# Attention scores of two heads: from 128-row products with moved halves to 64-row products in the two halves of the array

## The chip, the cores and the metric

The kernel runs on one core of a Trainium2 chip, as one launch. The metric is device time in microseconds (us), the median of several executions. TensorE (PE) multiplies matrices: it loads a stationary operand of up to 128 rows by 128 columns (LDWEIGHTS, listed as PEld) and streams a moving operand through it, into PSUM. VectorE (DVE), ScalarE (ACT) and GpSimd (POOL) do the rest, and DMA queues, most of them fed by SyncE (SP), move data.

## What is computed

Attention for 4 batches of 8 heads, 576 positions and 64 values per head, with a bias on the scores that a small network makes from positions; then a mixture of eight experts, in which each token goes to one expert.

```python
B, H, S, D = q.shape                      # 4, 8, 576, 64
scores = scale * np.matmul(q, k.transpose(0, 1, 3, 2))   # scale = 1/8
...
h = np.maximum(x @ w1 + b1, 0.0)          # x from positions alone
bias = h @ w2
scores = scores + bias.transpose(2, 0, 1)[None, :, :, :]
scores = scores - np.max(scores, axis=-1, keepdims=True)
attn = np.exp(scores)
attn = attn / (np.sum(attn, axis=-1, keepdims=True) + 1e-09)
return np.matmul(attn, v).astype(np.float32)
...
for e in range(E):                        # 8 experts, each token to one
    h = np.maximum(x[mask] @ w1[e], 0.0)
    ye = h @ w2[e]
    out[mask] = gate_w[mask, None] * eom[mask, e, None] * ye
```

## The kernel before

Heads are worked on in 16 pairs (batch b, pair pr of heads). The program has three stages. In the **bias stage** 36 steps (emit_hid, emit_bias) make the bias tiles: ACT and DVE make hidden rows (L724, L726), PE multiplies them (L737), ACT empties PSUM (L741) into one of four buffers, and SP writes those into the bias tiles by DMA (L747, L750). Table BEGIN (L66) hangs the first steps of pairs 0 to 2 on these 36 steps. Then comes the **attention stage**: FIRST (pair 0), ORDER (pairs 1 to 14) and LAST (pair 15) are strings that give the order of all steps by hand; one pass of the string serves one pair, a "-" after a step's name means the pair before, a "+" the pair after, "++" two after. Each engine does its instructions in the order in which the steps are emitted. At the end is the **expert stage** (body, from L1107): eight slots of 192 products.

The steps that matter here, for one pair:

- l (emit_load, L760): two DMAs bring keys and queries; each 128-column block of the tile nat has 64 key values and 64 query values of one head side by side.
- k0 k1 k2 (emit_kq, L800): three PE transposes each (L805) put keys in the upper 64 rows and queries in the lower 64. ACT writes the rounded part ("hi", with the scale 1/8 on the queries' rows, L808) and DVE the rest ("lo", L810).
- p0 p1 p2 (emit_place, L814): four DMAs of 288 KB inside the core move halves, so that the tile kt has the keys' hi in both halves, kl the keys' lo in both, and qs the queries' hi above their lo.
- s0 to s7 (emit_s, L842): scores of 128 queries of one head, by four products of 128 rows and 288 columns (L855): each contracts hi and lo of the queries at once, so four partial products go in two passes for each half of the columns. Then softmax_rows: one DVE instruction adds the bias and finds the row maximum (L835), and an ACT exponential follows (L840). The PSUM tile ps has two buffers, one per head.
- s8 (emit_s4, L862): the last 64 queries of both heads in one tile, by eight products (L871), from q4, which POOL fills (z, emit_q4).
- t (emit_t): transposes of the exponentials (L892, L904), emptied by ACT or DVE as the last letter says (L896, L907).
- a (emit_av, L909): twenty products with 64 stationary columns, whose outputs lie in the two column halves of the array (L924).
- w, u, x, y: pieces of routing, storing and of the experts' preparation.

## Time and profile before

| | us |
|---|---|
| median of 3 runs | 616.68 (616.17 to 617.11) |
| the profiled execution | 616.42 |
| its span | 614.5 |
| PE busy in the span | 575.9 |
| DVE busy | 413.7 |
| ACT busy | 375.0 |

The profiled execution took 1.9 us beyond its span and lies 0.26 us under the median. Busy time counts overlapping instructions once; a PE that is listed as busy may still be between two streams, so the start times of its instructions are read, not their durations.

### The profile page before, as it was taken

To read this page: it belongs to the slowest core of one execution; us is meant where nothing else is said; L and a number is where in the kernel's file an instruction comes from. 1 tells how busy PE (TensorE), PEld (TensorE's weight loads), DVE (VectorE), ACT (ScalarE), POOL (GpSimd) and SP (SyncE) were. 2 spreads that over 40 slices of the span, in tenths; PEclk is the share of its full clock that TensorE was granted. 3 is DMA by queue.
4 is the path that set the end of the run, shared out by engine and by line. 5 is a ranking of instruction groups with operands and counts; after the bars stand their busy time and mean duration, and the time that the engine had idled before them with its cause. 6 is when DMAs were issued, how large, how long until landed. Compare 5 with 4: busy or idle time off the path is not lost.

```text
span 614.5 us, 13532 instructions
## 1 busy us (share of the span) xinstructions
PE 575.9 (94%) x5070; PEld 489.2 (80%) x5070; DVE 413.7 (67%) x974; ACT 375.0 (61%) x774; POOL 96.1 (16%) x172
## 2 busy tenths in 40 slices
PE   4878789999999999999989999999999999999993
PEld 2323478887887788887778768999999999999993
DVE  6968756676786677786579765757778675555521
ACT  5778767777775677776776654545445454545510
POOL 1000000000001000100012372040404032230202
PEclk9979989999999999999999999999999999999997
DMA  6998975555656745676436666566656574757621
GB/s 139 228 206 209 219 159 121 130 127 110 142 127 169 169 102 107 134 192 148 103 88 158 190 209 207 158 221 198 209 173 213 169 215 159 232 163 215 187 73 47
DMA packets 99093, 100.26 MB, mean 163 GB/s; under 512 B 71319, under 2 KB 71575, under 8 KB 99016
## 3 DMA queue, kind: packets, MB, share of 16 engines
q1 hardware_dynamic: 93028, 84.93, 54.4%
q0 software_dynamic: 3232, 9.64, 5.0%
q10 hardware_dynamic: 2756, 4.72, 2.2%
q8 instruction: 42, 0.69, 0.5%
q14 instruction: 35, 0.29, 0.2%
HBM read 60.34 MB, written 9.50 MB: 114 GB/s over the span
## 4 chain that ended last, share of the span: by engine, by line
PE 79%; DVE 7%; DMA 5%; ACT 4%; issue 3%; POOL 0%; POOLq 0%; SPq 0%; DVEq 0%; ACTq 0%
PE p L1116 16%; PE p L1137 16%; PE pa L924 13%; PE ps L855 10%; PE pt L892 9%; PE pb L737 2%; DVE hid L726 2%; PE pt L805 2%; PE ps L871 2%; DMA bias<-evh 2%; DVE e L835 2%; PE pt L657 1%; PE pt L1156 1%; PE pt L904 1%; PE pt L515 1%
## 5 line engine op out<-in xcount | busy, mean ns | idle before, releaser
L840 ACT ACTIVATE e<-e,nm 128x576 f32<-128x576 f32 x144 | 111.3, 774 | 49.1 <-DVE nm L835 47.2
L835 DVE CUSTOM_DVE_ANT_0 e<-ps,bias 128x576 f32<-128x576 f32 x144 | 105.6, 751 | 31.1 <-PE ps L855 26.9
L1116 PE MATMUL p<-x,w 128*128 128x288 f32 x768 | 105.9, 297 | 0.0
L1116 PEld LDWEIGHTS p<-x,w 128*128 128x128 f32 x768 | 102.8, 188 | 0.5 <-issue 0.4
L892 PE MATMUL pt<-kept,e 128*128 128x128 f32 x576 | 82.7, 277 | 2.9 <-ACT et L896 1.2
L855 PE MATMUL ps<-qt,qs 128*128 128x288 f32 x256 | 80.0, 331 | 3.3 <-DVE nm L835 2.9
L892 PEld LDWEIGHTS pt<-kept,e 128*128 128x128 f32 x576 | 65.2, 141 | 17.8 <-issue 7.6
L1137 PE MATMUL p<-hh,w2h 128*128 128x288 f32 x256 | 77.3, 302 | 0.0
L1137 PE MATMUL p<-hl,w2h 128*128 128x288 f32 x256 | 75.6, 295 | 0.1
L1137 PE MATMUL p<-hh,w2l 128*128 128x288 f32 x256 | 75.3, 294 | 0.0
L924 PE MATMUL pa<-et,vt 128*64 128x256 f32 (+1 forms) x640 | 73.2, 354 | 0.0
L855 PE MATMUL ps<-kl,qs 128*128 128x288 f32 x256 | 71.4, 296 | 0.0
L896 ACT COPY et<-pt 128x512 f32<-128x512 f32 (+1 forms) x105 | 57.3, 565 | 12.1 <-PE pt L892 11.9
L737 PE MATMUL pb<-hid,w2blk 128*32 128x288 f32 x576 | 47.7, 442 | 17.6 <-DVE hid L726 8.3
L924 PEld LDWEIGHTS pa<-et,vt 128*64 128x64 f32 x640 | 42.6, 137 | 21.9 <-issue 6.1
L855 PEld LDWEIGHTS ps<-qt,qs 128*128 128x128 f32 x256 | 48.8, 191 | 7.2 <-DVE nm L835 4.5
L1118 ACT ACTIVATE hh<-p 128x288 fp32r<-128x288 f32 x64 | 26.3, 412 | 46.2 <-PE p L1116 28.4
L1081 POOL DMA_INDIRECT out_dram<-y,sidx x22 | 26.4, 1199 | 176.4 <-DVE y L1159 150.0
L737 PEld LDWEIGHTS pb<-hid,w2blk 128*32 128x32 f32 x576 | 19.0, 116 | 42.4 <-DVE hid L726 11.0
L726 DVE TENSOR_SCALAR hid<-e,early 128x576 f32<-128x576 f32 x110 | 48.5, 515 | 6.3 <-PE pb L737 2.8
L855 PEld LDWEIGHTS ps<-kl,qs 128*128 128x128 f32 x256 | 49.0, 191 | 0.0
L487 DVE TENSOR_TENSOR w2l<-w2r,w2h 128x1024 fp32r<-128x1024 f32 x32 | 39.2, 1226 | 14.2 <-ACT w2h L486 12.7
(218 smaller groups left out, 972.5 us busy)
## 6 DMA issues: line engine op xcount, KB each, us to landing
w1r<-in_moe_w_dram SPq DMA_DIRECT2D x36, 512.0 KB, 5.1
w2r<-in_moe_w_dram SPq DMA_DIRECT2D x36, 512.0 KB, 4.1
kl<-qs SPq DMA_DIRECT2D x32, 288.0 KB, 5.2
nat<-in_k_dram SPq DMA_DIRECT2D x16, 288.0 KB, 4.2
nat<-in_q_dram SPq DMA_DIRECT2D x16, 288.0 KB, 5.2
bias<-evh SPq DMA_DIRECT2D x16, 288.0 KB, 4.2
bias<-evl SPq DMA_DIRECT2D x16, 288.0 KB, 5.3
qs<-qt SPq DMA_DIRECT2D x16, 288.0 KB, 3.2
```

The source lines that it names most:

```text
L487: V.tensor_tensor(out=lo, in0=src, in1=hi.bitcast(F32), op=ALU.subtract)
L726: V.tensor_scalar(out=to, in0=src, scalar1=bc[:, r:r + 1], scalar2=0.0, op0=ALU.add, op1=ALU.max,)
L737: nc.tensor.matmul(pb[32 * t:32 * t + 32, c, 0:288], lhsT=w2f, rhs=hids[t][:, c * 288:c * 288 + 288], start=True, stop=True,)
L835: V.tensor_tensor_reduce(out=e.rearrange("p (a j) -> p a j", a=2), in0=ps[:, :, 0:n], in1=bias_ap.rearrange("p (a j) -> p a j", a=2), scal ...
L840: nc.scalar.activation(out=e, in_=e, func=ACTF.Exp, scale=-1.0, bias=nm, accum_out=sum_ap)
L855: nc.tensor.matmul(ps[:, c, 0:288], lhsT=qs[:, o:o + 128], rhs=keys[:, k0 + c * 288:k0 + c * 288 + 288], start=n == 0, stop=n == 1,)
L892: nc.tensor.transpose(pt[:, n * 256 + j * 128:n * 256 + j * 128 + 128], es[j][:, (n0 + n) * 128:(n0 + n) * 128 + 128], ident,)
L896: copy(out=et[:, n0:n0 + nn, :].rearrange("p n s -> p (n s)"), in_=pt[:, 0:nn * 256])
L924: nc.tensor.matmul(pa[p:p + 64, 0:n], lhsT=values, rhs=weights, start=i == 0, stop=i == 4)
L1081: p = nc.gpsimd.indirect_dma_start(out=out, out_offset=bass.IndirectOffsetOnAxis(ap=idx, axis=0), in_=y[0:n], in_offset=None, bounds_check ...
L1116: nc.tensor.matmul(p1[:, 0:CH], lhsT=w[:, fs], rhs=x[:, c, :], start=n == 0, stop=n == 11)
L1137: nc.tensor.matmul(p2[:, 0:CH], lhsT=w[f // 2][:, f % 2, ds], rhs=x[f], start=n == 0, stop=n == 23)
```

## The change

Keys and queries of the two heads now stand in different halves: the load puts both heads side by side, so that the transposes leave head 0 in rows 0 to 63 and head 1 in rows 64 to 127, keys and queries in different columns. Nothing needs to be moved after that, and emit_place with its four DMAs is gone. The loads are six DMAs for the same bytes. The scores are three products of 64 rows (hi x hi, hi x lo, lo x hi; lo x lo is dropped) for each half of the columns and each head, and those of head 0 and head 1 alternate. The last 64 queries stay products of 128 rows (q4 is block diagonal), six in place of eight. The scale 1/8 moves into the DVE instruction of the softmax, and the bias tiles are made 8 times larger.

The steps are cut anew: s0 to s3 are both heads of 128 queries and emit only the products; m0 to m3 emit the softmax of both; s4 and m4 are the last 64 queries; k0 to k2 emit transposes and hi, h0 to h2 emit lo. Keys are prepared for the next pair and not for the one after it. In the bias stage, the heads of pair 0 that are begun there are still done one at a time (s00, s10, s01, s11). Which engine empties a transpose changes for several t steps.

```diff
 ORDER = (
-    "s2 s1 c w u a0d- t10a- p0+ s3 u w t11a- s0 u t12a- s6 t20d- p1+ u s7 b- t04d u s8 t01d t03a u "
-    "t02a s5 s4 z+ u w w g- a1a- t14d u p2+ t13a t00d u k0++ a2a- v+ t21d u k1++ w k2++ u l+++ "
+    "l++ s0 b- c t10a- w t12a- m0 u t13d- k2+ s1 u t14a- m1 h2+ u t21d- a0d- w u w u w g- s2 z t20a- t01a t03a m2 u "
+    "t02d u a2d- w s3 u k1+ k0+ t00a m3 u s4 w m4 u t04a h1+ h0+ u a1d- v+ t11d u "
 )
 FIRST = (
-    "s4 t04d t01d s5 t03a t02a s6 t00d s7 v+ s8 t14d z+ k0++ t13a k1++ t21d k2++ l+++"
+    "l++ s2 z m2 t01a t03a t02d s3 m3 t00a v+ s4 m4 t04a t11d"
 )
 LAST = (
-    "b- B W s2 s1 c a0d- u t10a- w s3 u t11a- u s0 t12a- u s6 w t20d- s7 u g- t04d u t01d y t03a s8 u y "
-    "t02a a1a- y s5 X t00d w y s4 a2d- y t14d t13d y a0d t21d w y t12d u y t20d u "
+    "b- B W s0 c t10a- u w t12a- m0 u t13d- u s1 t14a- m1 u t21d- a0d- w u s2 z t20a- g- m2 a1a- u t01a t03a w u y "
+    "t02d u s3 y t00a m3 u X y t04d s4 y a2d- m4 w y t11d t13a y a0d u t14d t12a y y w t21d u t20d u "
 )
...
 BEGIN = {
-    3: "k0", 4: "k1", 5: "k2 l", 7: "p0", 9: "p1", 13: "p2 K0", 14: "z", 16: "K1", 17: "s0", 20: "K2",
-    21: "L", 22: "s2 s1", 29: "P0", 32: "s3 P1", 35: "v P2",
+    3: "k0", 4: "k1", 5: "k2 l", 13: "K0", 16: "K1", 17: "s00", 20: "K2",
+    22: "s10 s01", 32: "s11", 35: "v",
 }
...
-    c["cinv"] = np.stack([1.0 / psi[first + 4 * (q // NE)].astype(np.float64) for q in range(128)])
+    c["cinv"] = np.stack([8.0 / psi[first + 4 * (q // NE)].astype(np.float64) for q in range(128)])
...
         def emit_load(b, pr):
-            t = nat_t[b, pr] = nat.tile([128, 9, 2, D], F32, name="nat", tag="nat")
+
+            t = nat_t[b, pr] = (nat, kq)[pr % 2].tile([128, 9, 2, D], F32, name="nat", tag="nat")
             for i, x in enumerate((k, q)):
+                for hl in range(2):
+                    nc.sync.dma_start(
+                        out=t[:, 5 * i:5 * i + 4, hl, :],
+                        in_=x[b, 2 * pr + hl, 0:512].rearrange("(n p) d -> p n d", p=128),
+                    )
...
-            nc.scalar.activation(out=hi, in_=pt[:, 0:384], func=ACTF.Copy, scale=cn("ksc"))
-            yield
-            V.scalar_tensor_tensor(
-                out=lo, in0=pt[:, 0:384], scalar=cn("ksc"), in1=hi.bitcast(F32), op0=ALU.mult, op1=ALU.subtract
-            )
-
-        def emit_place(b, pr, i):
-
-            hi, lo = (t[(b * NPAIR + pr) % 2] for t in (kh2, qs2))
-            if i == 0:
-                kl_t[b, pr] = kq.tile([128, 2 * S], F32R, name="kl", tag="kt")
-            kl, up, down = kl_t[b, pr], slice(0, 64), slice(64, 128)
-            for to, src in (((kl[up], lo[up]), (kl[down], lo[up])), ((lo[up], hi[down]),), ((hi[down], hi[up]),))[i]:
-                nc.sync.dma_start(out=to.bitcast(F32), in_=src.bitcast(F32))
+            nc.scalar.copy(out=hi, in_=pt[:, 0:384])
+            yield
+            V.tensor_tensor(out=lo, in0=pt[:, 0:384], in1=hi.bitcast(F32), op=ALU.subtract)
...
+        def products(b, pr, qb, heads, outs):
+
+            high, low = (t[(b * NPAIR + pr) % 2] for t in (high2, low2))
+            for c in range(2):
+                for i, (t, keys) in enumerate(((0, high), (0, low), (1, high))):
+                    qs = (high, low)[t]
+                    for hl in heads:
+                        p = slice(hl * 64, hl * 64 + 64) if qb < 4 else slice(0, 128)
+                        nc.tensor.matmul(
+                            outs[hl][:, c, 0:288],
+                            lhsT=qs[p, S + 64 + qb * 128:S + 192 + qb * 128] if qb < 4 else q4[:, t, :],
+                            rhs=keys[p, c * 288:c * 288 + 288], start=i == 0, stop=i == 2,
+                        )
...
-                scale=-1.0, scalar=3.0e38, op0=ALU.add, op1=ALU.min, accum_out=nm,
+                scale=-0.125, scalar=3.0e38, op0=ALU.add, op1=ALU.min, accum_out=nm,
...
-        def emit_s(b, pr, qb, hl):
-            h = 2 * pr + hl
+        def emit_s(b, pr, qb, heads=(0, 1)):
...
             e_t[b, pr, qb] = e_all[qb]
...
+            ps = {hl: ps_s.tile([128, 2, 512], F32, name="ps", tag="s") for hl in heads}
+            products(b, pr, qb, heads, ps)
+            yield
+            for hl in heads:
+                h = 2 * pr + hl
+                softmax_rows(e_t[b, pr, qb][:, hl, :], ps[hl], bias[qb][:, h, :], sums_t[b][:, qb, h:h + 1])
```

## Rows read from the trace of the kernel before

**Rows 1.** Page, parts 1 and 4: busy time; the chain that ended last, by engine.

```profile
PE 575.9 (94%) x5070; PEld 489.2 (80%) x5070; DVE 413.7 (67%) x974; ACT 375.0 (61%) x774; POOL 96.1 (16%) x172
...
PE 79%; DVE 7%; DMA 5%; ACT 4%; issue 3%; POOL 0%; POOLq 0%; SPq 0%; DVEq 0%; ACTq 0%
```

**Rows 2.** The chain in order of time: start us, us, what; pair 1, then later pairs.

```profile
92.77 1.16 PE ps L871 x8
93.93 1.31 PE pt L892 x12
95.24 1.06 PE ps L855 x8
96.30 2.31 PE pa L924 x20
...
105.42 0.59 PE pt L892 x4
106.01 0.53 PE ps L855 x4
106.54 0.44 PE pt L892 x4
...
109.66 0.45 PE ps L871 x3
...
271.48 1.10 PE ps L871 x8
...
303.93 0.75 DVE e L835
...
352.55 1.05 PE ps L871 x8
```

**Rows 3.** Busy time by stretch: us, busy us (instructions) of each engine, clock, DMA.

```profile
core 0: us, PE busy (x) PEld busy (x) DVE busy (x) ACT busy (x) POOL busy (x), PEclk, DMA share, GB/s
92.77:109.66 16.89, 16.86 (x151) 14.11 (x152) 11.52 (x29) 12.76 (x30) 0.99 (x4) 1.00 0.61 132
...
0.00:84.00 84.00, 61.99 (x669) 30.50 (x669) 61.91 (x146) 62.12 (x102) 3.83 (x20) 0.95 0.87 198
...
30.50:35.50 5.00, 2.25 (x35) 0.78 (x28) 1.38 (x3) 2.78 (x5) 0.08 (x1) 0.94 0.69 159
35.50:42.00 6.50, 6.44 (x51) 2.26 (x51) 4.98 (x11) 5.51 (x9) 0.21 (x1) 0.52 1.04 232
```

**Rows 4.** Timeline: start us, us, engine, line, instruction: score products, then pa products.

```profile
201.76 0.30 PE L855 MATMUL ps<-qt,qs 128*128 128x288 f32 x1
201.76 0.19 PEld L855 LDWEIGHTS ps<-kl,qs 128*128 128x128 f32 x1
201.90 0.29 PE L855 MATMUL ps<-kl,qs 128*128 128x288 f32 x1
...
202.43 0.30 PE L855 MATMUL ps<-kl,qs 128*128 128x288 f32 x1
...
209.69 0.29 PE L855 MATMUL ps<-kl,qs 128*128 128x288 f32 x1
...
209.91 1.49 PEld L924 LDWEIGHTS pa<-et,vt 128*64 128x64 f32 x16 [0.17 <-issue]
```

**Rows 5.** Timeline: pa products of 64 columns in the array's column halves; then transposes.

```profile
207.20 0.14 PEld L924 LDWEIGHTS pa<-et,vt 128*64 128x64 f32 x1
...
207.20 0.22 PE L924 MATMUL pa<-et,vb 128*64 128x64 f32 x1
207.21 0.14 PEld L924 LDWEIGHTS pa<-et,vb 128*64 128x64 f32 x1
...
207.25 0.22 PE L924 MATMUL pa<-et,vt 128*64 128x64 f32 x1
...
207.26 0.22 PE L924 MATMUL pa<-et,vb 128*64 128x64 f32 x1
...
218.06 1.36 PEld L892 LDWEIGHTS pt<-kept,e 128*128 128x128 f32 x12
```

**Rows 6.** Timeline: softmax on DVE for two heads in turn; ACT empties a transposed tile.

```profile
210.10 0.75 DVE L835 CUSTOM_DVE_ANT_0 e<-ps,bias 128x576 f32<-128x576 f32 x1
...
210.77 0.75 DVE L835 CUSTOM_DVE_ANT_0 e<-ps,bias 128x576 f32<-128x576 f32 x1
...
217.04 0.57 ACT L896 COPY et<-pt 128x512 f32<-128x512 f32 x1
```

**Rows 7.** Waits from 0 to 84 us: us in total, times, longest.

```profile
ACT evh L741 <- DMA bias<-evh: 3.2, 3, 2.2
...
ACT evl L741 <- DMA bias<-evl: 1.4, 2, 1.1
...
SPq L821 <- DMA kl<-qs: 4.1, 1, 4.1
```

**Rows 8.** Timeline of the bias stage: the same 32 products at two speeds.

```profile
18.27 2.19 PE L737 MATMUL pb<-hid,w2blk 128*32 128x288 f32 x32
...
35.47 4.36 PE L737 MATMUL pb<-hid,w2blk 128*32 128x288 f32 x32 [0.78 <-ACT evh L741]
```

More of the change, by code (lines that the diff above doesn't have):

```diff
@@ L113, in _tables @@
     c["slot"] = np.tile(np.arange(NSLOT + 2.0), (128, 1))
-    c["ksc"] = np.where(p < 64, 1.0, 0.125)[:, None]
     psi = np.log1p(np.maximum(np.arange(S, dtype=np.float32), np.float32(1.0)))
@@ L551, in first_w2 @@
         load_w2(0)
-    kh2, qs2 = ([qx.tile([128, 2 * S], F32R, name=f"{t}{i}", tag=f"{t}{i}") for i in range(2)] for t in ("qt", "qs"))
-    q4 = qx.tile([128, 256], F32R, name="q4")
+    high2, low2 = ([qx.tile([128, 2 * S], F32R, name=f"{t}{i}", tag=f"{t}{i}") for i in range(2)] for t in ("qt", "qs"))
+    q4 = qx.tile([128, 2, 128], F32R, name="q4")
     wgb = const.tile([128, NPAIR, 32], F32, name="wgb")
@@ L800, in emit_kq @@
         def emit_kq(b, pr, c):
-            hi, lo = (t[(b * NPAIR + pr) % 2][:, c * 384:c * 384 + 384] for t in (kh2, qs2))
+            hi, lo = (t[(b * NPAIR + pr) % 2][:, c * 384:c * 384 + 384] for t in (high2, low2))
             pt = psum_t()
@@ new lines, in emit_q4 @@
+        def emit_q4(b, pr):
+            for i, t in enumerate((high2, low2)):
+                for hl in range(2):
+                    p = slice(hl * 64, hl * 64 + 64)
+                    nc.gpsimd.tensor_copy(
+                        out=q4[p, i, p], in_=t[(b * NPAIR + pr) % 2][p, S:S + 64].bitcast(F32)
+                    )
[10 more added lines that the diff above has]
+                            rhs=keys[p, c * 288:c * 288 + 288], start=i == 0, stop=i == 2,
+                        )
@@ L927, in attention_moe_kernel @@
         pairs = [(b, pr) for b in range(B) for pr in range(NPAIR)]
-        begun = " ".join(BEGIN.values()).split()
+        late, turned = {}, []
         def begin(op):
@@ L997, in copies @@
             return nc.scalar.copy if c == "a" else V.tensor_copy
-        to_act = ("t00", "t01", "t04", "t14")
+        to_act = ("t02", "t13")
         orders = {0: FIRST, len(pairs) - 1: LAST, len(pairs): END}
         for n in range(len(pairs) + 1):
-            todo = {i: 1 for i in range(8)}
             for op in orders.get(n, ORDER).split():
@@ L1023, in attention_moe_kernel @@
                     first_split(splits.pop(0))
-                if name in "wuxWBXy" or not 0 <= m < len(pairs) or m == 0 and name in begun or m == 1 and name[0] == "p":
+                if name in "wuxWBXy" or not 0 <= m < len(pairs) :
                     continue
@@ L1027, in attention_moe_kernel @@
                 i = int((name + "0")[1])
-                if name == "s8":
-                    emit_s4(b, pr)
-                elif name[0] == "s":
-                    finish(emit_s(b, pr, i // 2, i % 2))
-                    if m == len(pairs) - 1:
-                        todo.pop(i)
-                        if i > 5 and not any(j in todo for j in (6, 7)):
+                if name[0] in "sk":
+                    late[name] = emit_s(b, pr, i) if name[0] == "s" else emit_kq(b, pr, i)
+                    next(late[name])
+                elif name[0] in "mh":
+                    finish(late.pop({"m": "s", "h": "k"}[name[0]] + name[1]))
+                    if name[0] == "m" and m == len(pairs) - 1:
+                        if i == 3:
                             work.insert(0, first(first_w2))
-                        if i in (4, 5) and not any(j in todo for j in (4, 5)):
+                        if i == 2:
                             t = biasp.tile([128, 4, 4, CH], F32R, name="x", tag="bias2")
```

67 lines of the change are left out of this document (18 added, 49 removed).

## The prediction

> **What bounds the kernel now.** I read the page first, then the chain of waits in order of time, then busy time by stretch, and last the timeline of a few microseconds. The page puts PE at 94% busy and at 79% of the chain that ended last [rows 1]. The chain in order of time says where: from the first product of the last query tile of pair 1 to that of pair 2 (92.77 to 109.66, 16.89 us) every piece is PE, and the same steps come back until pair 11 begins at 271.48, ten periods of 17.87 us on average with the pieces of routing in them [rows 2]. In one such period DVE is busy 11.52 us and ACT 12.76 of 16.89, and the clock is granted in full [rows 3]. So for pairs 1 to 11 what shortens PE shortens the kernel. From pair 12 to 15 the period is 20.27 us ((352.55 - 271.48) / 4), and softmax instructions of DVE stand in the chain between PE's pieces [rows 2]: I count a PE saving there at half. The bias stage (0 to 84 us) has no engine busy for more than 62.12 of 84 us, while the DMA engines are busy 87% of the time [rows 3]: work and writes wait on each other. The expert stage is not touched.
>
> **Products of the scores.** Score products start 0.134 us apart: five intervals from 201.76 to 202.43 [rows 4]. I call one such time p = 0.133 (eight take 1.06 [rows 2]). Before, a pair of heads has 8 tiles of 4 products and one of 8: 40 x 0.133 = 5.32 us. After, it has 4 blocks of 6 pairs of half products, and one tile of 6 full ones. If the two halves of the array work at the same time, that is 24 x 0.133 + 6 x 0.133 = 3.99 us, 1.33 less. If they don't, it is 48 x 0.133 + 0.80 = 7.18, 1.86 more.
>
> No product in this trace uses row halves, so this price needs bounds. The nearest rows are the column halves of pa: two products start within 0.01 us of each other, so do their two weight loads, and a couple follows the next every 0.055 us [rows 5]. That is both at once, in loads and in streams. On the other side stand the loads of 128 columns, one every 0.113 us (12 in 1.36 [rows 5]): if the loads of the two halves queue up, a couple takes 2 x 0.113 = 0.226. The range is 0.113 (one load's pace, should a couple be bound by nothing else) to 0.266 (two products in turn). I take 0.133, since the row nearest to it, two halves with a load each, shows both at once.
>
> The Trainium skill ("TensorE: Matmul & The Clock Gate", Part 3, What overlaps and what doesn't) says that a weight load overlaps a running product only where their row groups differ. Here the load at 201.76 starts with the product before its own, on the same 128 rows, and the pace stays 0.134 [rows 4], so the trace doesn't bear this out for full rows. For half rows no run here shows it; it is weighed as a rival below. The same page gives a speedup of 3.07 for four row quarters of 32 rows; as an estimate from that figure alone, at 77% of ideal, a couple would take 0.173 us and the sum would come out near no change.
>
> **Changes of layout in the array.** A switch costs PE time. Into the column halves: 0.22 us between starts (209.69 to 209.91 [rows 4]) where products alone take 0.133, so 0.09. Out of them: four transposes take 0.59 directly after pa and 0.44 elsewhere, so 0.15 [rows 2]. For row halves I take the same: they are bounded by 0 (a half is no switch) and by twice that. Each of the 4 blocks pays it in and out, 4 x 0.24 = 0.96. Two blocks stand directly behind a pa step, which would have paid its way out anyway: -2 x 0.15. The old order has scores begin at seven places of a pass and the new one at five; I set these two starts against the uncertain length of a switch. So about +0.6 us per pair (0 to 1.3). **Net per pair: -1.33 + 0.6 = -0.73 us.** With 11 pairs in full and 4 at half, 13 x 0.73 = **-9.5 us**. Pair 0 I count at nothing: half its tiles are done singly and DVE and ACT set its end.
>
> **Waits that the new order adds.** A block needs both buffers of ps, so it can start in full only after both softmax instructions of the block before. The narrowest place is s0 to s1. DVE needs about 0.2 after the last product, then 0.67 + 0.75 (210.10 to 210.77, and one more [rows 6]) = 1.6 us. PE has in between t10, t12, t13 (12 transposes) and k2 (3): 15 x 0.11 = 1.65 us (0.44 for four [rows 2]) and 0.15 for the way out. It fits by 0.2 us. Where it fails, transposes behind s1, and with them ACT's copies, wait as well. Between the other blocks stand a pa step of 2.31 us [rows 2] or 10 transposes, more than one buffer needs. m0 stands ahead of t13's copy in DVE's queue, so this copy comes late, but its PSUM buffer is next wanted only after s1. Copies move to ACT: it empties eight t tiles where it emptied five, and two pa tiles fewer; at no more than 0.57 us a tile [rows 6] that is at most 1.7 us per pair, so ACT has at most 14.5 of about 16.1 us (12.76 of 16.89 before [rows 3]) and is not the bound. lo (h steps) is emitted later than hi and holds PSUM buffers longer, behind m4 for chunks 0 and 1; a pa step of 2.31 covers it. If that cover fails, up to 0.6 us per pair. q4 takes four POOL copies in place of one; POOL is busy 0.99 of 16.89 us [rows 3]. Keys one pair ahead move the work of three k steps from pair 0's pass to a later one: no change in the sum.
>
> **The transfers and the bias stage.** Eight of the placing DMAs fall in the first 84 us, and one pair's load goes out of it. ACT waits 3.2 + 1.4 = 4.6 us there for bias writes, 2.2 at one time, behind a placing DMA for which SP's queue stood still 4.1 us [rows 7]. PE is busy only 2.25 of 5.00 us around it, and then from 35.5 to 42 us the granted clock is 0.52, near the lower level of 1.2 GHz [rows 3]: 32 products take 4.36 us that took 2.19 earlier [rows 8]. I expect about 3.5 us of ACT's waits to go, some 1.5 of the 2.2 us that the slow stretch costs, and 1.1 to come on top for the four tiles done singly, six products in place of four (8 x 0.133). **-4 us**, between 0 (DVE, busy 61.91 [rows 3], is late next) and -12 (what is left if the stage keeps 10 us over its busiest engine). In the attention stage no wait of PE hangs on the placing, so its four DMAs per pair give nothing more, and the six loads take SP's time in their place.
>
> **Sum.** The profiled execution took 616.42: span 614.5 and 1.9 around it. 616.4 - 9.5 - 4 = 602.9; the median lay 0.26 above that execution, so I say 603.
>
> **Rivals.**
> A. The halves don't overlap (the change doesn't do what it says on PE). For it: no row of before shows row halves. Against: column halves do overlap [rows 5]. Place: each of the 24 couples; price: with queued loads 0.226 a couple, 24 x 0.226 + 0.80 + 0.6 - 5.32 = +1.5 per pair, 13 x 1.5 - 4 = +15.5, 632 us; in turn +2.46 per pair, +28, 644. It decides from p = 0.177 on, where 24p + 0.80 + 0.6 - 4/13 reaches 5.32.
> B. Each half's load waits for its own half's product: 0.113 + 0.133 = 0.246 a couple, +2.0 per pair, +22, 638 us. It would be the rule of the page named above. Against it stand rows 4 and rows 5. I give it 8 of 100, A 14.
> C. The halves overlap in part, p = 0.16 to 0.19: 24p is 3.84 to 4.56, net -0.1 to +0.6 per pair, 611 to 620 us.
> D. PE gains and DVE's or ACT's chain takes it: a stall of 0.2 to 0.5 us at s0 to s1 and before s4. For it: the margin of 0.2 us. Against: before, one softmax sets the next tile's start as well, and PE hardly waited for it in pairs 1 to 11. 606 to 612 us.
> E. The bias stage loses all its waits and switches are free: 13 x 1.33 + 12 = 29 less, 587 us.
>
> **How the numbers follow.** Forecast (598 to 607): 0.45. E: 0.06. D: 0.19. C: 0.08. A: 0.14, B: 0.08. The range leaves out the far end of E and most of A and B: 588 to 632. Differences under 0.2% (1.2 us) can't be told from no change. Faster: forecast, E, D, and half of C: 0.74. Same: 0.02, a quarter of C. Slower: 0.24, the rest.
>
> **What would show it.** In the timeline two score products, and two loads, start within about 0.02 us of each other, and a block of 12 takes about 0.8 us; if it takes 1.4 or 1.6, A or B holds. The first four transposes after a block take about 0.59 in the chain. A period of a pair without routing is near 16.1 us. If PE is idle before products with softmax as the releaser, it is D. In the first 84 us the waits of ACT for bias writes and the slow stretch should be gone, and the attention stage should begin some 4 us earlier. I am wrong if the period falls and the total doesn't, or if the stage from pair 12 on, which I only counted at half, grows.

## The result and the profile after

The changed kernel takes 623.78 us (median of five, 621.02 to 626.37) where the kernel before takes 616.68: 1.0111 times as long, 95% interval 1.0073 to 1.015. I had forecast 603. Its profiled execution took 626.37, span 624.6, 10.1 us more than the span of before; it is the longest of the five, 2.6 us above the median. The page of the changed kernel, part 1:

```profile
PE 580.3 (93%) x5294; PEld 472.9 (76%) x5294; DVE 410.8 (66%) x975; ACT 362.0 (58%) x773; POOL 105.6 (17%) x220
```

Beside [rows 1] all engines look alike, and PE is even busy a little longer (580.3 us in place of 575.9). So the page doesn't show the loss; the starts of the passes do. I took the start of the first score product of each pass from both timelines (profiled executions):

| stretch | before, us | after, us | difference |
|---|---|---|---|
| up to pass 2 (bias stage, pairs 0 and 1) | 101.8 | 98.5 | -3.3 |
| passes 2 and 3 (no routing) | 33.7 | 33.3 | -0.4 |
| passes 4 to 7 (routing of batch 0) | 73.2 | 74.9 | +1.7 |
| passes 8 to 11 (routing of batch 1) | 72.2 | 75.0 | +2.7 |
| passes 12 and 13 | 42.4 | 42.5 | +0.1 |
| pass 14 | 17.8 | 22.6 | +4.9 |
| pass 15, to the first expert product | 30.4 | 34.6 | +4.2 |
| experts | 243.0 | 243.2 | +0.2 |

**The half products do what the change says.** Timeline of PE, first products of pass 8 after the change ("x2" joins two that start together):

```profile
206.71 0.40 PE L833 MATMUL ps<-qt 64*128 64x288 f32 x2
206.94 0.29 PE L833 MATMUL ps<-qs,qt 64*128 64x288 f32 x2
207.08 0.29 PE L833 MATMUL ps<-qt,qs 64*128 64x288 f32 x2
207.21 0.30 PE L833 MATMUL ps<-qt 64*128 64x288 f32 x2
```

A couple follows the next every 0.13 us, the pace of one full product in [rows 4]. Yet a pass without routing only went from 16.86 to 16.63 us. Chain in order of time of the changed kernel, pass 2:

```profile
98.00 0.59 PE pt L886 x4
98.58 0.99 PE ps L833 x12
99.57 1.46 PE pt L886 x12
...
102.90 2.31 PE pa L918 x20
105.21 1.00 PE ps L833 x12
106.21 0.59 PE pt L898 x4
...
111.15 0.84 PE ps L833 x6
...
115.22 0.85 PE ps L833 x9
```

Six full products of the last score tile take 0.84, six couples 0.98 to 1.00, and the transposes behind a block 0.15 more than elsewhere (x4 0.59 against 0.44, x12 1.46 against 1.31 in [rows 2]).

**The loss lies where routing pieces are worked in.** (These are short pieces of work of the routing, w in the strings, u as well from pass 12 on.) Busy time by stretch, after: a pass without routing, pass 4, passes 8 to 11, pass 14; then before, pass 14 and passes 8 to 11:

```profile
core 0: us, PE busy (x) PEld busy (x) DVE busy (x) ACT busy (x) POOL busy (x), PEclk, DMA share, GB/s
...
115.20:131.80 16.60, 16.60 (x167) 12.75 (x166) 11.28 (x28) 11.71 (x29) 1.57 (x7) 1.00 0.29 63
131.80:152.00 20.20, 19.25 (x188) 13.91 (x187) 13.37 (x35) 12.52 (x32) 1.62 (x7) 1.00 0.25 54
206.70:281.70 75.00, 73.06 (x712) 54.72 (x711) 52.98 (x138) 48.59 (x122) 7.63 (x35) 1.00 0.30 72
324.10:346.80 22.70, 19.98 (x195) 15.05 (x194) 17.57 (x55) 13.08 (x31) 6.72 (x17) 1.00 0.18 51
```

```profile
323.30:341.10 17.80, 17.58 (x163) 14.51 (x161) 14.58 (x48) 12.90 (x30) 4.11 (x11) 1.00 0.58 140
...
208.70:280.90 72.20, 72.06 (x655) 59.53 (x654) 53.74 (x138) 52.38 (x123) 5.23 (x23) 1.00 0.61 140
```

Taken against four passes without routing (4 x 16.86, 4 x 16.63), the pieces cost 4.8 us before and 8.5 after. In passes 8 to 11 PE was idle 0.14 us before and 1.94 after; the rest of the difference is time in which PE is listed as busy. In pass 14 VectorE has 3.0 us more to do (the key steps of pair 15, which were done in pass 13, and more pieces) and PE is idle 2.7 us in place of 0.2. The timeline of pass 4 after, from the end of the value step a0, shows such a place:

```profile
137.86 0.60 PE L918 MATMUL pa<-et,vz 128*64 128x256 f32 x4
...
138.39 1.22 PE L588 MATMUL pt<-xt,wgb 128*32 128x256 f32 x8
138.51 0.42 DVE L919 COPY xt<-pa 128x256 f32<-128x256 f32 x1 [0.59 <-PE pa L918]
...
139.65 0.37 ACT L611 COPY ls<-pt 128x256 f32<-128x256 f32 x1 [1.27 <-PE pt L588]
...
140.07 0.44 PE L618 MATMUL pt<-kept,ls 128*128 128x128 f32 x2 [0.46 <-ACT ls L611]
140.44 0.40 PE L833 MATMUL ps<-qt 64*128 64x288 f32 x2
```

Two routing pieces stand with no other work of PE between them: the logits (L588) need a copy by VectorE of what PE has only just made, and their transposes (L618) a copy by ScalarE. Part of these waits is listed as busy: the eight logit products take 1.16 us in the chain here, since the last two stand behind the copy, and 0.57 in pass 4 of the kernel before, where scores stand between:

```profile
140.21 0.57 PE pt L588 x8
```

The third block comes 5.8 us after the second; in pass 2 it is 3.8.

**The last pass** waits for a transfer in this execution. Chain, and busy time by stretch:

```profile
366.00 8.34 DMA xg<-x_dram,gidx
...
374.38 0.90 PE pt L515 x4
375.28 4.47 PE pa L918 x20
```

```profile
374.40:381.40 7.00, 7.00 (x51) 4.32 (x51) 1.85 (x5) 1.51 (x4) 3.49 (x3) 0.57 0.78 270
```

The last of the first three gathers takes 8.34 us; PE waits for the tokens 0.42 and 1.95 us, and after this idle time the granted clock is 0.57 for 7 us, near the lower of the two levels (1.2 and 2.4 GHz): a value step takes 4.47 us in place of 2.31. The load of w2r (2 MB) is issued at 362.40, the gathers at 363.43 to 366.00; in the kernel before the load goes out at 351.53 and PE doesn't wait.

### The profile page after: what moved, and what is told of

The parts are those of the page before. It is cut to its first block, busy times and chain, and to the rows that moved or that the text cites. A ratio compares the mean times of both kernels' runs of the same rounds, so it can differ in the third digit from the quotient of the medians.

```text
span 624.6 us, 13990 instructions
## 1 busy us (share of the span) xinstructions
PE 580.3 (93%) x5294; PEld 472.9 (76%) x5294; DVE 410.8 (66%) x975; ACT 362.0 (58%) x773; POOL 105.6 (17%) x220
## 4 chain that ended last, share of the span: by engine, by line
PE 79%; DVE 6%; DMA 4%; ACT 4%; issue 3%; POOL 2%; SPq 1%; POOLq 0%; DVEq 0%; ACTq 0%
PE p L1102 16%; PE p L1123 16%; PE pa L918 14%; PE ps L833 10%; PE pt L886 9%; PE pb L737 4%; PE pt L810 2%; DMA bias<-evl 2%; PE pt L515 1%; PE pt L1142 1%; PE pt L898 1%; PE pt L657 1%; DMA xg<-x_dram,gidx 1%; DVE hid L726 1%; DVE e L845 1%
## 5 line engine op out<-in xcount | busy, mean ns | idle before, releaser
L845 DVE CUSTOM_DVE_ANT_0 e<-ps,bias 128x576 f32<-128x576 f32 x144 | 103.9, 754 | 40.1 <-PE ps L833 34.6
L886 PE MATMUL pt<-kept,e 128*128 128x128 f32 x576 | 84.1, 280 | 3.6 <-DVE x L666 2.5
L890 ACT COPY et<-pt 128x512 f32<-128x512 f32 (+1 forms) x117 | 59.8, 534 | 42.4 <-PE pt L886 41.0
L886 PEld LDWEIGHTS pt<-kept,e 128*128 128x128 f32 x576 | 62.6, 141 | 20.0 <-issue 9.9
L918 PE MATMUL pa<-et,vt 128*64 128x256 f32 (+1 forms) x640 | 74.9, 360 | 0.0
L737 PE MATMUL pb<-hid,w2blk 128*32 128x288 f32 x576 | 47.9, 459 | 16.7 <-DVE hid L726 7.5
L833 PE MATMUL ps<-qt 64*128 64x288 f32 x256 | 47.8, 344 | 2.9 <-DVE nm L845 2.0
L1123 PEld LDWEIGHTS p<-hh,w2h 128*128 128x128 f32 x256 | 48.0, 188 | 0.6 <-issue 0.6
L1123 PEld LDWEIGHTS p<-hl,w2h 128*128 128x128 f32 x256 | 48.1, 188 | 0.3 <-DVE hl L1105 0.3
L1123 PEld LDWEIGHTS p<-hh,w2l 128*128 128x128 f32 x256 | 48.2, 188 | 0.0
```

Of the source, the lines that this page charges most:

```text
L737: nc.tensor.matmul(pb[32 * t:32 * t + 32, c, 0:288], lhsT=w2f, rhs=hids[t][:, c * 288:c * 288 + 288], start=True, stop=True,)
L833: nc.tensor.matmul(outs[hl][:, c, 0:288], lhsT=qs[p, S + 64 + qb * 128:S + 192 + qb * 128] if qb < 4 else q4[:, t, :], rhs=keys[p, c * 288 ...
L845: V.tensor_tensor_reduce(out=e.rearrange("p (a j) -> p a j", a=2), in0=ps[:, :, 0:n], in1=bias_ap.rearrange("p (a j) -> p a j", a=2), scal ...
L886: nc.tensor.transpose(pt[:, n * 256 + j * 128:n * 256 + j * 128 + 128], es[j][:, (n0 + n) * 128:(n0 + n) * 128 + 128], ident,)
L890: copy(out=et[:, n0:n0 + nn, :].rearrange("p n s -> p (n s)"), in_=pt[:, 0:nn * 256])
L918: nc.tensor.matmul(pa[p:p + 64, 0:n], lhsT=values, rhs=weights, start=i == 0, stop=i == 4)
```

## Experiments

### What the half products are worth

In turn: all products of head 0, then all of head 1.

```diff
-            for c in range(2):
-                for i, (t, keys) in enumerate(...):
-                    for hl in heads:
+            for hl in heads:
+                for c in range(2):
+                    for i, (t, keys) in enumerate(...):
```

> The changed kernel, but in each block the six products of head 0 come first and then the six of head 1, so that half products of different halves no longer alternate. If the two halves work at the same time only because they alternate, a block takes 12 x 0.133 = 1.6 us of streams in place of 0.8, and the kernel loses about 15 passes x 4 blocks x 0.8 = 48 us (some 670 us). If a half's weight load has to wait for its own half's product (0.113 + 0.133 = 0.246 a product), a block takes about 3.0 us and the kernel loses 130 us. If the alternation gains nothing, the time stays near 624.

Measured: 639.26 us (one execution), between the forecasts. Timeline of PE, first block of pass 2:

```profile
98.64 0.40 PE L833 MATMUL ps<-qt 64*128 64x288 f32 x1
98.88 0.29 PE L833 MATMUL ps<-qs,qt 64*128 64x288 f32 x1
99.01 0.29 PE L833 MATMUL ps<-qt,qs 64*128 64x288 f32 x1
99.02 0.41 PE L833 MATMUL ps<-qt 64*128 64x288 f32 x2
...
99.51 0.29 PE L833 MATMUL ps<-qt 64*128 64x288 f32 x1
```

Three products of one head run alone, then the other head's first starts beside the fourth: the halves run as if each had a queue of its own, in which one gets about three products ahead here. Products of one half alone follow each other in 0.13 us, so their loads are hidden: rival B has nothing for it here. A block takes 1.14 us from its first to its last start in place of 0.8, and a pass without routing 18.1 in place of 16.6.

Full rows: 8 products on 128 rows per block, in the new order. This kernel leaves out the split of the rows.

```diff
+            if qb < 4:
+                for hl in heads:
+                    for c in range(2):
+                        for i, keys in enumerate((high, low)):
+                            nc.tensor.matmul(outs[hl][:, c, 0:288],
+                                lhsT=(high, low)[hl][:, S + 64 + qb * 128:S + 192 + qb * 128],
+                                rhs=keys[:, c * 288:c * 288 + 288], start=i == 0, stop=i == 1)
+                return
```

> This kernel leaves out the split into halves and computes other scores: each block of two heads is 8 products on all 128 rows (4 per head, the count of the kernel before), in the changed kernel's order, with its transfers and its emission of softmax; the score tile of the last 64 queries is left as it is. So it is the new order without the new products. Theory (a change between full rows and row halves costs about 0.19 us on the way in and 0.15 on the way out, which eats nearly all of the 1.33 us that couples save): a block of 8 takes 1.06 to 1.14 us with no such price, against 0.98 to 1.00 and 0.15 behind two of four blocks, so a pass without routing takes 16.5 to 17.0 us where the changed kernel takes 16.63, and the whole is within 4 us of the changed kernel (620 to 628). Then the products are worth nothing net and what is lost against the kernel before is lost by the order. Rival (the products save 0.73 us a pass as I forecast, and something in the order hides it): a pass gets 0.5 to 0.7 us longer, the whole 630 to 634 us.

Measured: 624.78 us (ratio 1.0125, 1.0077 to 1.0174), a pass without routing 16.7. The new order loses the same with the old kind of product. The same edit again, on the best version found below (low earlier, 609.56 us):

> The run low earlier (609.6 us, hardly any wait left in the attention stage) with 8 products on all 128 rows in each block of two heads in place of 6 couples of half products; it computes other scores, everything else stays. So it is what the half products are worth where no wait hides it. Theory (a block of couples takes 0.98 to 1.00 in the chain and makes the transposes behind it 0.15 longer; a block of 8 full products takes 1.06 to 1.10 and makes none longer): a pass without routing 16.5 to 16.7 us against 16.5, the whole 609 to 612.5. Rival (my forecast, net 0.73 us a pass): 17.2 us a pass, the whole 618 to 620.

Measured: 609.45 us (0.9904, 0.987 to 0.9939). Chain of one pass with full rows:

```profile
100.50 1.07 PE ps L832 x8
101.58 0.22 PE pt L896 x2
...
104.21 1.25 PE ps L832 x8
105.46 0.44 PE pt L908 x4
```

and with half products, the same places:

```profile
102.01 0.99 PE ps L833 x12
103.00 0.37 PE pt L886 x2
...
105.78 0.99 PE ps L833 x12
106.77 0.59 PE pt L898 x4
```

Behind transposes a block of couples saves 0.08 us and gives back 0.15 in the transposes that follow; behind a value step, where full products pay 0.18 for the change from column halves too, it saves 0.26. That is 3 x 0.26 + 0.08 - 4 x 0.15 = 0.26 us a pass, of which 0.15 is lost at the last score tile (0.84 us, and 0.33 for its transposes; with full rows 0.80 and 0.22). The period is 16.52 against 16.65 us (98.67 to 115.19, 97.05 to 113.70): 0.13 us per pass, under what the total can show.

One block cut in two by transposes (S2 is its second half of columns), so one change of layout in and out more per pass:

```diff
-g- s2 z t20a- t01a t03a m2 u
+g- s2 z t20a- S2 t01a t03a m2 u
```

> The changed kernel with one switch of the array's layout doubled: in passes 1 to 14 the block of query tile 2 is cut in two, and the four transposes t20 stand between its halves. If a switch costs 0.19 us in and 0.15 out, as the chain of the changed kernel suggests, that is 14 x 0.34 = 4.8 us more (about 0.8%), and the two halves of the block take some 0.59 us each in the chain in place of 0.99 in one. If switches cost nothing and the lost gain went elsewhere, the time stays within 1 us.

Measured: 624.6 us (1.0138, 1.0103 to 1.0174). A pass without routing takes 16.87 in place of 16.63, passes 2 to 14 together 250.6 in place of 248.2. So 0.24 us for both changes in the undisturbed pass where 0.34 was expected: the two halves take 0.18 more than one block, but the twelve transposes behind go only from 1.39 to 1.46, since they had lost 0.08 (against 1.31) already. In passes 5, 9, 13 and 14, which have waits, nothing of it is left, and the total, 0.8 us above the changed kernel, can't tell it from nothing.

The first block directly behind a1, the transposes t11 moved behind its softmax:

```diff
-t12a- m0 u t13d- k2+ s1
+t12a- m0 u t11d- t13d- k2+ s1
...
-u a1d- v+ t11d u
+u a1d- v+ u
```

> The transposes t11 move from the end of a pass behind the first block's softmax in the next, so this block stands directly behind the value step a1, and a third of the four blocks has a change from column halves to row halves in place of one from full rows, and the transposes behind a value step pay no way out. Theory (each change of layout has its price of 0.15 to 0.19 us): a pass without routing gets 0.15 to 0.3 us shorter (16.35 to 16.5), the whole 2 to 4 us. Rival (the price of 0.34 belongs to a block, whatever stands ahead of it): within 0.1 us a pass, within 1.5 us in all. Should the cover between the first and the second block have been short, it has 0.4 us more.

Measured: 622.92 us (1.0098, 1.0067 to 1.0129): 0.1 us less in a pass without routing (16.5), 0.3 more in passes 7 and 11; on the total nothing can be told.

### Is it the order?

The old order of steps, one head at a time with full rows, but with the change's loads, keys one pair ahead and bias stage:

```diff
-    "l++ s0 b- c t10a- w t12a- m0 u t13d- k2+ s1 u t14a- m1 h2+ ...
+    "l++ s2 s1 c z w u a0d- t10a- s3 u w t11a- s0 u t12a- s6 ...
```

> This kernel computes other scores (4 products on all 128 rows per head, taken one head at a time, the last score tile as six products) and keeps the six loads, the missing placing transfers, the keys one pair ahead and the bias stage of the change; only the step order and the places of softmax, copies and routing pieces are those of the kernel before. So it is the change without the new order. Theory (the order costs: softmax of two heads together, and PSUM buffers of the key steps held until their low part is taken off behind the next block's softmax, make PE wait wherever routing pieces come in): no loss in the passes with routing, passes 4 to 7 about 72 us together (73.2 before, less 0.27 a pass for the last tile), pass 14 18-19 us, the first expert product 4 to 8 us earlier than in the kernel before, the whole 609-613. Rival (the loss comes with the transfers or with the keys one pair ahead, whose work now falls into passes 12 to 14): passes 4 to 7 near 75 and pass 14 near 22, the whole 618 or more.

Measured: 621.58 us (1.0102, 1.0066 to 1.0138). The total missed, for a reason of this kernel's own: the keys come one pair ahead at the very end of a pass, and the next scores wait for ScalarE's hi part once a pass, 11 times up to the start of pass 12, 6.4 us. Busy time by stretch, a pass without routing and passes 8 to 11:

```profile
112.80:130.10 17.30, 16.73 (x148) 13.81 (x148) 11.35 (x29) 12.28 (x29) 1.63 (x7) 1.00 0.27 61
204.20:278.30 74.10, 71.77 (x646) 58.64 (x646) 53.20 (x139) 50.66 (x122) 7.93 (x35) 1.00 0.30 73
```

Routing adds 74.1 - 4 x 17.35 = 4.7 us to four passes, as in the kernel before (4.8), where the new order adds 8.5; and PE is idle in them as long as in four passes without routing (2.3 us), so the waits for hi hide nothing of the routing. So it is the order, not transfers or keys, that makes routing dear. Pass 14 took 19.7 us: at most 2.0 of the 4.9 come with the keys of pair 15, 2.9 with the order.

### Which wait of the order?

I moved the routing pieces (w) of a pass three times by rules that each missed. First behind the transposes of the third block:

```diff
-a0d- w u w u w g- s2 z t20a- t01a t03a m2 u t02d u a2d- w s3 u k1+
+a0d- u u g- s2 z t20a- w t01a t03a w m2 u t02d w u a2d- s3 w u k1+
```

> The changed kernel with the pieces of routing and storing (w) moved in passes 1 to 14: the three behind the first pa step and the one behind the last query tile's pa step now stand behind transposes or scores, so that their input is ready; their number stays six a pass. If PE loses its time by waiting for a copy of pa and for the logits' copy there (0.39 + 0.45 + 0.46 us in pass 4), the passes that begin a batch's routing (4, 8, 12) shrink by 1 to 2 us each and pass 14 by some, 4 to 7 us in all. If the pieces cost their own PE time wherever they stand, the time stays within 1 us.

Measured: 627.35 us (1.0171, 1.0112 to 1.0231). Pass 4 is unchanged (20.3), passes 5 and 6 are 0.9 and 1.0 us longer. The pieces now stood ahead of a softmax on VectorE, and the next block, which needs both buffers of ps, waited half-way: 13 waits of PE for a softmax, 5.3 us, where the changed kernel has 3 and 1.2 us (96 to 346 us). Then behind each softmax:

```diff
-c t10a- w t12a-
+c t10a- t12a-
...
-m1 h2+ u t21d- a0d- w u w u w g- s2 z t20a- t01a t03a m2 u t02d u a2d- w s3
+m1 h2+ w u t21d- w a0d- u u g- s2 z t20a- t01a t03a m2 w u t02d w u a2d- s3
...
-m3 u s4 w m4 u t04a h1+ h0+
+m3 w u s4 m4 u t04a w h1+ h0+
```

> Only the places of the routing pieces (w) in a pass change: none stands between a block's products and its softmax, and none directly behind another one or behind a product step of the values; each has transposes or products behind it. In the changed kernel three of them stand in a row between the first value step and the third block, and in pass 4 PE waits there 0.52 us for the copy of its own operand and 0.46 us for ScalarE's copy, and the third block starts 2.1 us later than in a pass without routing. Theory (these rows of waits, and routing pieces ahead of softmax on VectorE, cost 1.3 to 2.2 us in each of passes 4, 6, 8 and 10 and part of the 4.9 us in pass 14): passes 4 and 6 fall from 20.2 to 18.3-18.9 us, the whole by 4 to 8 us, to 616-620. Rival (VectorE's total work in these passes sets their length, wherever the pieces stand): within 1.5 us of the changed kernel.

Measured: 649.9 us (1.0532, 1.0502 to 1.0562). Waits of PE from 96 to 346 us (us in total, times, longest):

```profile
PE pt L657 <- ACT et L890: 9.4, 8, 2.6
PE pt L618 <- ACT ls L611: 6.1, 4, 1.6
```

Behind a softmax of two heads ScalarE has two exponentials in its queue (0.79 + 0.77 us of work, 0.2 behind each), and the copies that empty pt come after them. Behind the idle time the granted clock fell to 0.93 in the profile's pass 6. Then five to a pass, some 3 us apart:

```diff
+m0 w u t13d- u k2+ s1 t14a- m1 h2+ w u t21d- u a0d- g- s2 z t20a- t01a t03a m2 w u t02d u a2d- s3
+k1+ k0+ t00a m3 w u s4 m4 u t04a h1+ w h0+ u a1d- v+ u t11d
```

> Only the places of the routing pieces (w, u) change: five w in a pass in place of six, ten u in place of twelve (as many as the kernel before has), each directly behind the softmax of a block, some 3 us apart on PE. The run before this one with pieces behind the softmax (work behind) had them 0.4 to 1.0 us apart, and there PE waited up to 1.7 us for ScalarE, whose queue had the two exponentials of a block (2.0 us together) ahead of the copy that the next piece's transposes read. Theory (a block of two heads puts 1.4 us on VectorE and 2.0 on ScalarE in one piece; a routing piece costs PE nothing as long as none stands ahead of a softmax and its partner comes over 3 us later): passes 4 to 7 take 71.5-73.5 us together in place of 74.9, passes 8 to 11 the same, pass 14 20-21 in place of 22.6; part of the routing goes on in the last pass. The whole 5 to 8 us below the changed kernel: 615-619. Rival (VectorE's work in sum sets these passes): passes 4 to 7 within 0.7 us of 74.9, the whole within 2 us of the changed kernel.

Measured: 628.31 us (1.0198, 1.0158 to 1.0237); with the last pass exchanged (below) 626.22, where 612 to 617 was expected. Passes 4 to 7 took 78.0 us (with 3.5 us at a granted clock of 0.51) and 76.4: missed again. With the first block behind a1 as well:

> As the run beside it, and the first block directly behind the value step a1 (alone this took 0.1 us off a pass without routing, but passes 7 and 11 got 0.3 longer). Theory (one change of layout less per pass): 0.1 us per pass, 0.5 to 1.5 us less than the run beside it. Rival: within 0.5 us of it, or slower, where the transposes t11 now stand among the routing pieces.

Measured: 622.66 us (1.0092, 1.0056 to 1.0129). Beside 4.4 us of waits for ScalarE's copies, PE waited up to 1.3 and 0.9 us (twice each) for "DVE qs L815": the pieces want a buffer of pt (there are three), and the low part of a key step, emitted behind the next softmax, still held it. So the next version kept pieces out of the way between a key step and its low part:

```diff
+m0 u t11d- t13d- w k2+ s1 t14a- m1 h2+ u w t21d- u a0d- u g- s2 z t20a- t01a t03a m2 u w t02d u a2d- w s3
+k1+ k0+ t00a m3 s4 m4 t04a h1+ h0+ u w u a1d- v+ u
```

> The changed kernel with the last pass exchanged, the first block behind a1, and five routing pieces to a pass, none of which stands between a key step and the low part that releases its buffer: there the run with pieces five apart showed PE waiting 1.3 and 0.9 us for a buffer that the low part (the subtraction on VectorE) held. Theory (three PSUM buffers are shared by transposes, key steps and routing pieces, and PE waits for them, not for operands): passes 4 to 7 take 70.5-73 us together in place of 74.9, passes 12 to 14 take 62-64 in place of 65.1, the whole 612-618. Rival (the waits move to the next place, as in the three runs before that moved pieces): 75 us or more, the whole 620-624.

Measured: 617.69 us (1.0026, 1.0007 to 1.0044). Passes 12 to 14 fell from 65.1 to 60.7 us, passes 4 to 7 stayed at 75.1. Two pieces still came right behind a low part, and the waits of PE said for whom:

```profile
PE pt L657 <- DVE qs L815: 2.2, 2, 1.1
PE pt L588 <- DVE qs L815: 2.1, 2, 1.0
PE pt L618 <- ACT ls L611: 1.7, 2, 0.8
...
PE pt L630 <- DVE qs L815: 1.1, 1, 1.1
PE pt L266 <- DVE qs L815: 1.1, 1, 1.1
```

From there two ways. Pieces directly ahead of blocks, four to a pass:

```diff
+k2+ s1 w t14a- m1 h2+ u t21d- u a0d- w u g- s2 z t20a- t01a t03a m2 u t02d u a2d- w s3
+k1+ k0+ t00a m3 s4 m4 t04a h1+ h0+ u u a1d- v+ w u
```

> As the run clear of keys (617.7 us), with four routing pieces to a pass in place of five, directly ahead of the first, third and fourth block and behind the products of the second, so that none is emitted between a key step and its low part and none directly behind the softmax of a block. In the run clear of keys PE still waits in passes 4 to 7 0.8 us for ScalarE's copy of the logits behind two exponentials and 1.03 us for a buffer that the low part of the keys holds. Theory (these two kinds of wait are what routing costs in the new order): both go, passes 4 to 7 take 71.5-73.5 us together (75.1 there, 73.2 in the kernel before), the whole 612-616, below the kernel before. Rival (whatever the place, a piece on VectorE delays a softmax that the next block needs with both heads): 74.5 or more, the whole 616-619.

Measured: 615.1 us (0.9965, 0.9943 to 0.9988), passes 4 to 7 72.3; the last pass paid part of it back (a wait of 3.5 us in leftover routing). And the low parts earlier, the pieces left where they were:

```diff
-k1+ k0+ t00a m3 s4 m4 t04a h1+ h0+ u w u a1d-
+k1+ k0+ t00a m3 h1+ h0+ s4 m4 t04a u w u a1d-
```

> As the run clear of keys, with only the low parts of the second and third key step taken off directly behind the softmax of the fourth block and no longer behind the softmax of the last score tile, so their two PSUM buffers come free about 0.8 to 1.5 us earlier. Theory (buffers held by the low parts make PE wait): the waits of routing pieces for the low part (2.2 + 2.1 + 1.1 + 1.1 us over the attention stage) halve, the whole 1 to 3 us less than the run clear of keys. Rival (VectorE is the limit, in whatever order): within 0.7 us of it, and the last score tile's softmax, now 1.0 us later, makes the next pass's first block wait.

Measured: **609.56 us (0.9889, 0.9861 to 0.9916)**, 1.1% under the kernel before and 2.3% under the changed one. Waits of PE, 96 to 346 us, all that are left over 0.2:

```profile
PE pt L618 <- ACT ls L611: 1.7, 2, 0.8
PE pt L810 <- DVE et L890: 1.3, 3, 0.9
PE ps L833 <- DVE nm L845: 0.3, 1, 0.3
```

The 6.5 us of waits for L815 are gone, passes 8 to 11 take 72.7 us, and passes 2 to 14 take 236.5 in place of 243.9. The edit changes nothing else, so the buffers held by the low parts were the cause there. Alone in the changed kernel:

```diff
-t00a m3 u s4 w m4 u t04a h1+ h0+ u a1d-
+t00a m3 h1+ h0+ u s4 w m4 u t04a u a1d-
```

> The changed kernel with one edit alone: the low parts of the second and third key step are taken off directly behind the softmax of the fourth block, and no longer behind that of the last score tile and the transposes t04. In the run low earlier this edit was worth 8.1 us on top of three others. Theory (buffers of PSUM that low parts hold are what the routing pieces wait for, and in the changed kernel a piece stands exactly between, behind the last score tile): 3 to 8 us less than the changed kernel, 616-621, the gain in passes 4, 6, 8, 10 and 12 to 14. Rival (the edit pays only where the pieces are five apart; in the changed kernel three pieces in a row ahead of the third block are the wait): less than 1.5 us.

Measured: 618.03 us (1.0020, 0.9997 to 1.0044), 5.7 under the changed kernel; passes 2 to 14 take 243.5 in place of 248.2 us, of it 0.6 to 1.0 less in each of passes 4, 6, 8 and 10. Two rows of waits of the changed kernel (96 to 346 us) are gone with it:

```profile
PE pt L886 <- DVE x L666: 2.5, 3, 0.8
PE pt L886 <- DVE lt L632: 0.8, 2, 0.4
```

All five are waits of the transposes t04 behind the last score tile. Two of the three buffers of pt hold key steps there, and the third a routing piece, so t04 waits until VectorE has emptied the piece. What low only leaves is the place with two pieces in a row: in pass 4 the third block still comes 5.8 us after the second. Last, low earlier with two pieces moved once more:

```diff
-t13d- w k2+ s1 t14a- m1 h2+ u w t21d- u a0d- u g- s2 z
+t13d- k2+ s1 w t14a- m1 h2+ u t21d- u a0d- u g- s2 w z
```

> As the run low earlier (609.6 us), with the first two routing pieces of a pass moved: one from between t13 and the key step to behind the second block's products, one from behind the low part of the first key step to behind the third block's products, so the copy of the logits stands ahead of two exponentials on ScalarE and no longer behind them. Theory: the waits of 0.84 us for this copy and of 0.9 us for a copy ahead of the key step go, once or twice in every four passes: 2 to 4 us less, 605.5 to 608. Rival: a piece on VectorE ahead of a softmax delays the next block by as much: 609 to 611.

Measured: 610.24 us (0.9889, 0.9863 to 0.9915), no better than low earlier: the rival's number held. The waits of 1.7 and 1.3 us that it aimed at are gone, but PE now waits 1.4 us for another copy by ScalarE and 1.0 for a softmax.

### The last pass

The third and fourth block (s2, s3 and their softmax) exchanged in LAST, so that the tile that w2r takes over is free earlier:

```diff
-s2 z t20a- g- m2 a1a- u t01a t03a w u y t02d u s3 y t00a m3 u X y
+s3 z t20a- g- m3 a1a- u t01a t03a w u y t02d u s2 y t00a m2 u X y
```

> The changed kernel with the blocks of query tiles 2 and 3 exchanged in the last pass alone, so that the bias tile of tile 3, whose place the first weights w2 take, comes free some 6 us earlier. If the load of w2 (2 MB) collides with the gathers of the first expert's rows, these now land some 4 us after the third is issued, where they took 8.3, and the kernel gains about 4 us. If the gathers are late because GpSimd and ScalarE are behind with splitting w1, nothing changes (within 1 us).

Measured: 621.31 us (1.0065, 1.0049 to 1.0082), its executions 620.5 to 621.5 where the changed kernel has 621.0 to 626.4. The load goes out at 356.36, the gathers from 362.71; PE doesn't wait, and the last pass takes 29.3 us. The opposite, the load behind the gathers:

```diff
-                        if i == 3:
+                        if i == 4:
                             work.insert(0, first(first_w2))
```

> Only one thing changes: the load of the first second-layer weights (4 x 512 KB) goes in work behind the softmax of the last score tile and no longer behind that of query tile 3, so it is issued after the gather of the first tokens and not together with it. Theory (load and gather share the transfers' time; PE waits for the gathered tokens, and where it waits long enough the granted clock falls in the next 10 us): the gathers take 2 to 4 us in place of 8, PE has no wait for them over 0.3 us, the last pass takes 29-31 us in every execution, the whole 619-622 with less spread than the changed kernel (621 to 626). Rival (the gather is late by itself, since its indices or the GpSimd queue are late): gathers still land at 374 us or later and nothing changes.

Measured: 623.14 us (1.0096, 1.0061 to 1.013). The edit missed its aim: the load still went out first, at 364.51, the gathers from 365.53, since GpSimd had a piece waiting for ScalarE ahead of them. PE waited 2.7 us. So an early load takes the wait away. In the profiled executions of all 20 kernels: where the load goes out 1.0 to 1.5 us ahead of the first gather, PE waits for the tokens 0.5 to 2.7 us in eight of nine executions; where it goes out 5.9 us ahead or more, in none of ten; in one it goes out behind the first two gathers, and PE doesn't wait. Whether gather and load compete for the transfers or the gather is merely late was not separated.

## Why the prediction was wrong

**Products: right.** p is 0.13; rivals A, B and C fell.

**Changes of layout: under-sized.** I took 0.09 for the way in, from [rows 4], and 0.15 for the way out. The chain shows 0.18 to 0.20 in (0.98 to 1.00 for six couples at 0.133) and 0.15 out. Four times 0.34, less two ways out that the value steps had paid, is 1.06, where I had 0.6 with bounds to 1.3: net -0.27 by the chain, and -0.2 measured (16.86 to 16.63), in place of -0.73. Over the 13 passes of my sum that is 6.5 us of the forecast. And with full rows in the same order the period is only 0.10 to 0.13 longer. The rest of the -0.2 comes with the order; that it is the last tile's six products in place of eight (0.27) I argue only.

**New waits: the step that failed.** I named the place, "lo (h steps) is emitted later than hi and holds PSUM buffers longer, behind m4 for chunks 0 and 1; a pa step of 2.31 covers it", and priced it at nothing. That holds in passes without routing, such as the one that I weighed (92.77 to 109.66): PE doesn't wait there. In the others routing pieces stand exactly there and need those buffers. Taking the low parts off ahead of the last score tile is worth 5.7 us in the changed kernel (4.7 of it in passes 2 to 14 of the profiled executions) and 8.1 in the better one. I had put the cover's failure at 0.6 us per pair at most. Rival D had the sign and the engines, VectorE and ScalarE, but the wrong place (s0 to s1, which fits) and 606 to 612.

**Pieces (w, u): not in the sum.** I weighed the new order for its own steps and left the routing pieces between them out, though the string has six w in place of five, three of them in a row. They cost 8.5 us in four passes where they had cost 4.8. Place and buffers belong together: passes 2 to 14 take 248.2 us in the changed kernel, 243.5 with the low parts early alone, 243.9 with the pieces moved alone (clear of keys, five w to a pass, first block behind a1) and 236.5 with both, where the kernel before takes 239.3.

**Passes 12 to 15: wrong in sign.** I credited half of a gain there. Passes 12 and 13 gained nothing, pass 14 lost 4.9 (in part through the keys one pair ahead, for which I had written "no change") and pass 15 4.2 in the profiled execution, which is an unlucky one: with the same late load the last pass took 30.0 us in the run with pieces behind transposes and 30.5 in that with the cut block, against 30.4 before. I hadn't followed this load: it hangs on the softmax of query tile 3, and the new LAST does that tile fourth.

**Bias stage: -4 forecast, -3.3 measured at pass 2.** About 1.2 us of that (0.80 + 0.41 in the chain) is the key steps of one pair, now done later. The slow stretch didn't go, it moved. Busy time by stretch, after:

```profile
35.50:42.00 6.50, 4.64 (x61) 2.41 (x57) 4.71 (x12) 5.89 (x11) 0.00 (x0) 1.00 0.67 186
...
48.00:54.00 6.00, 4.15 (x30) 2.38 (x34) 2.12 (x6) 3.41 (x8) 0.00 (x0) 0.61 0.29 82
```

Where [rows 3] have a clock of 0.52 there is 1.00 now; but the chain has 3.10 us for a bias write at 43.79 and then VectorE, PE stands idle for 1.71 us up to 48.99, and from 48 to 54 us the clock is 0.61.

**The whole.** The profiled execution took 23.5 us more than the 602.9 of my sum. About 6.5 of it are the changes of layout, 4.7 the buffers held by low parts, 4.2 the last pass and 0.7 the bias stage. Most of the other 7 lies in passes 4 to 14, where moving the pieces, with the low parts early, takes 7.0 us off (243.5 to 236.5, of it 0.1 a pass through the first block behind a1). So the forecast of a gain failed by what it left out, and the size of its main term was wrong besides.

A count of mine was off, without consequence: ScalarE emptied six t tiles in a pass of the kernel before, not five. It has eight now and two fewer of pa, and is busy 11.71 us in a pass where it was busy 12.76.

## What to carry to other kernels

A step order is not priced by its own steps in an undisturbed pass alone: take the passes in which other work is slipped in, list who holds each shared PSUM buffer at those places and which queue must run before it is released. Two such faults can hide each other: here the cure of either took 4 to 5 us off passes 2 to 14, both together 11.7. Release a buffer (here by the subtraction that reads it last) before the next long pair of instructions on the same engine. And half-array products in short runs hardly pay: here a run of six couples saves 0.27 us of streams and pays up to 0.34 for changes of layout.

## What was new about the hardware

- Row halves of the array take products at 0.13 us per couple, the pace of one full product, loads of 64 rows included; issued in turn, one half ran about three products ahead of the other.
- A change between full rows and row halves takes 0.18 to 0.20 us in and 0.15 out; one from column halves to full rows 0.18 (a block of eight 1.25 behind a value step, 1.07 behind transposes). One change in and out more per pass made a pass 0.24 us longer.
- After waits of 2.4 us of PE in the last pass the granted clock was 0.57 for the next 7 us: a value step in it took 2.2 us longer, nearly as much again as the waits.
